# Query tiles 3 and 4 turned by way of DRAM and VectorE, and layer one's last blocks stored from ScalarE's queue

## The chip, the cores and the metric

The kernel runs on one core of a Trainium2 chip. Its time is the device time of one execution in microseconds. Engines are TensorE (PE, with its weight loads PEld), VectorE (DVE), ScalarE (ACT), GpSimd (POOL) and SyncE (SP). SP, ACT and POOL each have a queue from which they issue DMAs.

## The reference, cut to what matters

Two layers, each an attention block and a gated MLP, with the same weights in both. S = 2048 rows, D = 512, H = 32 heads of 16, Fh = 896; everything is float32.

```python
def _A_ref(x, wqkv, wo):                       # linear attention
    q, k, v = ...                              # heads of x @ wqkv
    phi = lambda t: jnp.where(t > 0, t + 1, jnp.exp(t)) + 1e-6
    pq, pk = phi(q), phi(k)
    kv = jnp.einsum("bhsd,bhse->bhde", pk, v)
    z = jnp.einsum("bhsd->bhd", pk)
    num = jnp.einsum("bhqd,bhde->bhqe", pq, kv)
    den = jnp.einsum("bhqd,bhd->bhq", pq, z)[..., None] + 1e-6
    return heads_joined(num / den) @ wo
def _B_ref(x, w_in, w_sp, b_sp, w_out):        # gated MLP over the sequence
    z = _gelu(jnp.einsum("bsd,df->bsf", x, w_in))
    z1 = z[..., :Fh]; z2 = _layernorm(z[..., Fh:], axis=-1)
    g = jnp.einsum("ts,bsf->btf", w_sp, z2) + b_sp[None, :, None]
    return jnp.einsum("bsf,fd->bsd", z1 * g, w_out)
x = x + _A_ref(_layernorm(x), ...)
x = x + _B_ref(_layernorm(x), ...)
x = x + _A_ref(_layernorm(x), ...)
x = x + _B_ref(_layernorm(x), ...)
```

## The kernel before

The sequence is cut into 16 tiles of 128 rows. A float32 product is made of three faster ones: every operand is split into a high part (an ACT copy, `high`, L220) and a low part (a VectorE subtraction, `low`, L223), and `mm3` (L234 to L236) multiplies high by high, high by low and low by high. So each product waits first for high parts and, from the second or third matmul on, for low parts.

Each layer L has four stages: P1 (keys, queries, the sums over the sequence), P2 (steps `s` over the tiles: the attention's output, the second layer norm, the MLP's first product), P4 (the product with `w_sp`, in seven sub-products P1 to P7 after Strassen) and the product with `w_out`. "Layer one" is L = 0 and "layer two" L = 1.

The order of each engine's instructions is the order in which the code issues them; there is no scheduler. Buffers are pools of numbered slots (`pages` of 128 x 512, 22 of them; `quads`; `bigs`; PSUM `banks`), handed out first in, first out. A DMA's queue also keeps order: an issue that waits holds back all behind it on its engine.

Query tiles pass through `Turn`, the class that transposes a tile. In P2, step s makes `a2_mul(s + 2)` (the divided queries, L877), stores that tile into the turn (`store`), and `b_high(s)` takes the turned tile out again, splits it, and `c(s)` multiplies it one step later. `c2` (L911) adds the product to x; `c3` stores x (L917) and normalises it (L378). `d_high`, `d_low` turn and split the normalised x tile in the same way, and `e` multiplies it.

A turn has two ways. For tiles in `by_pe`, ACT copies the tile with its features regrouped (L421), and TensorE transposes it in four matmuls against an identity into a PSUM bank (L390). For the others SP stores the tile into DRAM (L426), SP loads it in another order (L202, issued by `qturn.load`), and VectorE transposes 32 x 32 blocks into a page (L455). `by_pe` of the query turn also decides which steps of `run` and `run2` take the first branch of the step (those with the late query products of stage P1 in them).

At the end of P2, `tail` computes the last blocks of the activated half z1 (`out`, L1151: a GELU on ACT, then a store of the block, L1153) in three groups of three, and `yield`s between them; P4 starts in those gaps: at each yield it splits a weight block of `w_sp` (`wsp`: L1775 on ACT, L1778 on VectorE) and the z operand (L1883 or L220), and its products are L2000 to L2002. The store's engine is the argument `by`; without it, it is SP in layer one and POOL in layer two.

Of the kernel before, what the change touches and what calls it, by code (L numbers as in the profile page):

```python
# [19 lines left out]
NT = S // P  # L20
# [138 lines left out]
def mixer_kernel(ctx: ExitStack, tc: tile.TileContext, x_in, wqkv, wo_d, win1_d, win2_d, wsp_d, bsp_d, wout_d,  # L159
                 ident_d, mask_d, out_d):  # L160
    nc = tc.nc
# [76 lines left out]
    class Weight:  # L238


        def __init__(self, slots, shape, pieces, turned=False):
            self.slots, self.shape, self.pieces, self.turned = slots, shape, pieces, turned
            self.h = self.l = None
            self.raw = deque()
            self.n_load = self.n_split = 0
# [40 lines left out]
    def w_in1():  # L286
        return Weight(bigs, [P, NF, 4, P], [win1_d[f] for f in range(NF)])
# [543 lines left out]
    class P2:  # L831
        def __init__(self, p1):
            self.L = L = p1.L
            self.p1 = p1
            self.win1, self.win2 = None if L else w_in1(), p1.win2
            self.ws = deque()
            self.wf = deque([] if not L else [w1parts[f] for f in list(range(NF)) * 2 + [0, 6, 1, 2, 6]]
                            + [w1sums[f, m] for m in range(2) for f in range(3)]
                            + [[t[:, 256:512] for t in w1parts[f + 3]] for f in range(3)])
            self.draw, self.S, self.fdone, self.qhome, self.zacc, self.meant = {}, {}, None, {}, {}, set()  # L840
            self.qturn, self.xturn = Turn(f"qt{L}", range(5), True), Turn(f"yt{L}", (0, 1, 2, 3, NT - 1), home=ZHome, copy=bool(L))
            self.qp, self.qT, self.x, self.ms, self.xB, self.z, self.zms = {}, {}, {}, {}, {}, {}, {}
            self.fq = deque()
            self.fnext = []
            self.A, self.u, self.y = {}, {}, {}
# [388 lines left out]
        def tail(self):  # L1234
            V, A = nc.vector, nc.scalar.activation
            h, l = (t.bitcast(F32) for t in self.xT[3])
            L = self.L
            big = [bigs.get([P, NF, 512], F32R if k < 2 else F32) for k in range(3 if L else 2)]
            if L:
                c = [big[2][:, f] for f in range(3)]  # L1240
                room = Rooms(big[2][:, f] for f in range(3, NF))
            else:
                c = [pages.get(PAGE) for _ in range(3)]
                room = pages
# [13 lines left out]
            ws, d = [], []  # L1258
# [40 lines left out]
                V.tensor_add(c[f], d[f], c[f])  # L1299
            yield  # L1300
            for f in range(3):
                self.out(3, f + 3, c[f], c[f])
            x = [t[:, 2:4] for t in self.xT[3]]
            for f in range(3):
                self.fmul(self.y[f], [t[:, 256:512] for t in ws[f]], x, False, True)
# [1 line left out]
            quads.put(*self.xT.pop(3))  # L1307
            yield
            for f in range(3):
                self.out(3, f, self.y[f], room)  # L1310
                banks.done(self.y[f])
            for i in (NT - 2, NT - 1) if L else ():
                _, rs, nb = self.zms.pop(i)
# [7 lines left out]
                self.win1.free()  # L1321
            yield
            for f in range(3):
                self.out(2, f + 3, d[f], by=nc.sync)
                banks.done(d[f])
            bigs.put(*big)
            if not L:
# [2 lines left out]
        def run(self, sums):  # L1330
# [4 lines left out]
            for s in range(1, NT + 3):  # L1335
                if s in (15, 16, 17):
                    self.first_a(s - 15)
                self.loadx(s + 1)
                if s in self.qturn.by_pe:
                    self.c(s - 1)  # L1340
                    self.b_high(s)
                    self.c2(s - 1)
                    self.p1.late_phi_b()
                    self.b_low(s)
                    if s >= 2:
                        self.d_high(s - 2)
                        self.d_low(s - 2)
                    self.p1.late()
                    self.c3(s - 1)
                    self.a2(s + 2)  # L1350
                    self.p1.late_phi_a()
                    self.a(s + 3)
                    sums.tick()
                else:
                    if s < NT:
                        self.b_high(s)
                    self.a2_den(s + 2)
                    if s < NT:
                        self.b_low(s)
                    if s <= NT:  # L1360
                        self.c(s - 1)
                        self.c2(s - 1)
                    if s == NT:
                        quads.put(*self.W2)
                        pages.put(self.zbc)
                    self.a2_mul(s + 2)
                    late = s - 2 in self.xturn.by_pe and s <= NT or AHEAD <= s <= NT
                    if s in (NT, NT + 1):
                        self.e(s - 3)
                        self.e2(s - 3)  # L1370
                    if late:
                        self.d_high(s - 2)
                        self.d_low(s - 2)
                    if s <= NT:
                        self.c3(s - 1)
                    self.a(s + 3)
                    if s <= NT + 1 and not late:
                        self.d_high(s - 2)
                        self.d_low(s - 2)
# [99 lines left out]
        def run2(self):  # L1479
            late = self.p1  # L1480
            for s in range(1, NT + 3):
# [2 lines left out]
                self.qturn.load(s + 1)  # L1484
                if s in EXTRA:
                    self.wfetch()
                if s in self.qturn.by_pe:
                    self.c(s - 1)
                    self.b_high(s)
                    self.c2(s - 1)  # L1490
# [988 lines left out]
```

## Time and profile before

| | |
|---|---|
| median of 3 runs | 1342.88 us (1342.65 to 1342.91) |
| the profiled execution's own time | 1341.83 us |
| its span, first to last instruction | 1340.1 us |
| TensorE busy | 1334.2 us (100%), 6533 matmuls |
| VectorE busy | 1074.3 us (80%) |
| ScalarE busy | 739.8 us (55%) |
| GpSimd busy | 464.1 us (35%) |
| SP's and ACT's DMAs, share of 16 DMA engines | 56.2% |

Times in a row of a timeline are its start in us from the span's start, then its duration; "x8" behind it means eight merged instructions, and square brackets hold the idle time of the engine before it and what ended it. A row of grouped forms gives line, engine, operation, output<-input, form, count, busy us, mean ns of one, and idle time before. A row of waits gives the total, the number of times and the longest. Matmuls overlap: their durations are longer than the step from one start to the next, so the steps are read from the starts.

### The profile page before, as it was taken

The page shows a single profiled execution, that of the slowest core. Times are in us where ns is not written, and L with a number is a line of the kernel's source. Part 1 is how long each engine was busy: PE and PEld are TensorE (multiplying, and loading weights), DVE is VectorE, ACT ScalarE, POOL GpSimd, SP SyncE. Part 2 cuts the span into 40 slices and gives each one's busy share as a digit, 9 for nine tenths or more (in the row PEclk, how much of TensorE's full clock was granted, in tenths as well). Part 3 has the DMA queues.
Part 4 walks back from the last instruction along what each step waited for, and adds up shares of the span by engine and source line. Part 5 has one row for each costly group of instructions (what it writes and reads, how often), then busy time and mean ns, then how long its engine had stood idle before and what let it go on. Part 6 is the DMA issues. An engine that isn't in the chain of part 4 may idle for free.

```text
span 1340.1 us, 19243 instructions
## 1 busy us (share of the span) xinstructions
PE 1334.2 (100%) x6533; PEld 1138.6 (85%) x6533; DVE 1074.3 (80%) x1687; ACT 739.8 (55%) x1250; POOL 464.1 (35%) x611
## 2 busy tenths in 40 slices
PE   9999999999999999999999999999999999999998
PEld 7888888888888888889988888888888888888898
DVE  7779877767899889898866777777689758899885
ACT  5774544347742265345666655557687333666464
POOL 3765675533036400301422443544441012122021
PEclk9999999999999999999999999999999999999999
DMA  5898489977779986884864552678767455579354
GB/s 184 281 313 275 166 286 313 306 223 250 250 270 378 324 263 216 287 302 79 184 159 138 137 131 88 211 237 269 226 203 246 155 171 174 178 242 322 115 78 65
DMA packets 172594, 291.34 MB, mean 217 GB/s; under 512 B 14544, under 2 KB 53456, under 8 KB 172240
## 3 DMA queue, kind: packets, MB, share of 16 engines
q1 hardware_dynamic: 153376, 250.92, 56.2%
q0 software_dynamic: 18976, 39.07, 13.7%
q8 instruction: 51, 0.84, 0.3%
q14 instruction: 47, 0.39, 0.1%
q10 hardware_dynamic: 144, 0.13, 0.0%
HBM read 205.39 MB, written 101.45 MB: 229 GB/s over the span
## 4 chain that ended last, share of the span: by engine, by line
PE 95%; DMA 2%; DVE 2%; ACT 1%; issue 0%; POOL 0%; SPq 0%; DVEq 0%; ACTq 0%
PE bank L234 13%; PE bank L236 13%; PE bank L235 13%; PE bank L2001 12%; PE bank L2000 12%; PE bank L2002 12%; PE bank L2198 3%; PE bank L2199 3%; PE bank L2200 3%; PE bank L990 1%; PE bank L991 1%; PE bank L992 1%; PE bank L1163 1%; PE bank L1162 1%; PE bank L1161 1%; PE bank L390 1%
## 5 line engine op out<-in xcount | busy, mean ns | idle before, releaser
L2001 PE MATMUL bank<-qd,pg 128*128 128x512 f32 x736 | 286.5, 389 | 0.6 <-DVE qd L1778 0.6
L2002 PE MATMUL bank<-qd,pg 128*128 128x512 f32 x736 | 286.3, 389 | 0.0
L2000 PE MATMUL bank<-qd,pg 128*128 128x512 f32 x736 | 286.3, 389 | 0.0
L1775 ACT ACTIVATE qd<-qd 128x1024 fp32r<-128x1024 f32 x142 | 149.2, 1053 | 125.2 <-PE bank L2002 101.7
L1778 DVE TENSOR_TENSOR qd<-qd,qd 128x1024 fp32r<-128x1024 f32 x132 | 168.6, 1279 | 37.6 <-ACT qd L1775 37.4
L236 PE MATMUL bank<-qd,pg 128*128 128x512 f32 x448 | 174.7, 390 | 0.0
L2001 PEld LDWEIGHTS bank<-qd,pg 128*128 128x128 f32 x736 | 138.1, 188 | 29.5 <-DVE qd L1778 1.0
L2002 PEld LDWEIGHTS bank<-qd,pg 128*128 128x128 f32 x736 | 138.1, 188 | 28.8
L2000 PEld LDWEIGHTS bank<-qd,pg 128*128 128x128 f32 x736 | 138.1, 188 | 28.6
L2041 POOL TENSOR_TENSOR bg<-bg,pg 128x512 f32<-128x512 f32 x28 | 49.8, 1780 | 187.6 <-ACT qd L1775 92.5
L234 PE MATMUL bank<-qd,pg 128*128 128x512 f32 x264 | 103.2, 391 | 0.3 <-ACT pg L220 0.2
L235 PE MATMUL bank<-qd,pg 128*128 128x512 f32 x264 | 102.9, 390 | 0.0
L236 PEld LDWEIGHTS bank<-qd,pg 128*128 128x128 f32 x448 | 84.1, 188 | 18.2 <-DVE pg L223 0.4
L1684 POOL TENSOR_TENSOR pg<-pg,pg 128x512 f32<-128x512 f32 x48 | 70.8, 1476 | 68.7 <-DMA pg<-in_wsp_dram 66.6
L369 POOL TENSOR_SCALAR rs<-mv 128x1 f32<-128x1 f32 x76 | 23.8, 313 | 172.7 <-DVE mv L367 169.0
L2200 PE MATMUL bank<-wo,qd 128*128 128x256 f32 x288 | 81.5, 283 | 0.0
L2198 PE MATMUL bank<-wo,qd 128*128 128x256 f32 x276 | 78.1, 283 | 0.0
L2199 PE MATMUL bank<-wo,qd 128*128 128x256 f32 x276 | 78.0, 283 | 0.0
L220 ACT ACTIVATE pg<-pg 128x512 fp32r<-128x512 f32 (+1 forms) x86 | 50.0, 592 | 45.8 <-DVE pg L1869 19.9
L223 DVE TENSOR_TENSOR pg<-pg,pg 128x512 fp32r<-128x512 f32 (+1 forms) x84 | 54.5, 657 | 11.3 <-ACT pg L220 10.6
L549 POOL TENSOR_TENSOR pg<-pg,pg 128x512 f32<-128x512 f32 x30 | 39.9, 1331 | 55.8 <-DVE pg L543 53.9
L234 PE MATMUL bank<-bg,qd 128*128 128x448 f32 x160 | 59.0, 369 | 0.0
(297 smaller groups left out, 3358.2 us busy)
## 6 DMA issues: line engine op xcount, KB each, us to landing
qd<-s SPq DMA_DIRECT2D x62, 512.0 KB, 4.6
qd<-in_wsp_dram SPq DMA_DIRECT2D x40, 512.0 KB, 4.0
qd<-hP SPq DMA_DIRECT2D x40, 512.0 KB, 4.6
pg<-z SPq DMA_DIRECT2D x56, 256.0 KB, 5.1
pg<-in_wsp_dram SPq DMA_DIRECT2D x52, 256.0 KB, 4.4
s<-pg SPq DMA_DIRECT2D x48, 256.0 KB, 4.0
z<-pg SPq DMA_DIRECT2D x40, 256.0 KB, 3.5
pg<-w POOLq DMA_DIRECT2D x38, 256.0 KB, 4.9
```

Source lines behind the costliest of these rows:

```text
L234: nc.tensor.matmul(out, ah, bh, start=start, stop=False)
L235: nc.tensor.matmul(out, ah, bl, start=False, stop=False)
L236: nc.tensor.matmul(out, al, bh, start=False, stop=stop)
L1684: nc.gpsimd.tensor_tensor(t, a, b, op=OP.add)
L1775: self.mark = nc.scalar.activation(w[:, 0], r, AF.Copy)
L1778: nc.vector.tensor_sub(w[:, 1], r, w[:, 0].bitcast(F32))
L2000: m(out, h[:, o], w[:, 0, j, :], start=start, stop=False, skip_group_check=True)
L2001: m(out, h[:, o], w[:, 1, j, :], start=False, stop=False, skip_group_check=True)
L2002: m(out, l[:, o], w[:, 0, j, :], start=False, stop=stop, skip_group_check=True)
L2198: m(out, A, x, start=start and f == 0, stop=False, skip_group_check=True)
L2199: m(out, A, y, start=False, stop=False, skip_group_check=True)
L2200: m(out, B, x, start=False, stop=stop and f == 2, skip_group_check=True)
```

## The change

The query turn's `by_pe` goes from tiles 0 to 4 to tiles 0 to 2 in both layers. The two loops' branch, which hung on `by_pe`, now hangs on `s < 5` (the last pair of lines below, in `run` and in `run2`), so the steps keep their order. In layer one, all nine stores of the tail are issued by ACT in place of SP; layer two keeps POOL and SP.

```diff
-            self.qturn, self.xturn = Turn(f"qt{L}", range(5), True), ...
+            self.qturn, self.xturn = Turn(f"qt{L}", range(3), True), ...
...
             for f in range(3):
-                self.out(3, f + 3, c[f], c[f])
+                self.out(3, f + 3, c[f], c[f], None if L else nc.scalar)
...
-                self.out(3, f, self.y[f], room)
+                self.out(3, f, self.y[f], room, None if L else nc.scalar)
...
-                self.out(2, f + 3, d[f], by=nc.sync)
+                self.out(2, f + 3, d[f], by=nc.sync if L else nc.scalar)
...
-                if s in self.qturn.by_pe:
+                if s < 5:
```

Three places show what moves. In the rows, `pg`, `qd`, `bg` are slots of pages, quads and bigs with running numbers; `qt_3` is the DRAM tile of query tile 3, `x_0` the stored x tile 0, `s_...` stored sums of `w_sp`, `z_0_2_3` a stored block of z1.

VectorE in layer one, step 3, from `a2_mul(4)` on, before:

```order
L877 SCALAR_TENSOR_TENSOR pg_196_1754<-z_q_674,den 128x512
L911 TENSOR_TENSOR pg_191_1693<-pg_191_1693,bank_69_1856 128x512
L365 BN_STATS st<-pg_191_1693 128x6
L367 BN_AGGR mv<-st 128x2
L531 SCALAR_TENSOR_TENSOR z_q_1839<-bank_68_1816,z_q_1839 128x512
L223 TENSOR_TENSOR pg_211_1887<-bank_70_1869,pg_210_1874 128x512
```

and with the change:

```order
L877 SCALAR_TENSOR_TENSOR pg_195_1754<-z_q_674,den 128x512
L455 STREAM_TRANSPOSE pg_210_1873<-pg_199_1766 128x4x128
L911 TENSOR_TENSOR pg_191_1693<-pg_191_1693,bank_69_1860 128x512
L365 BN_STATS st<-pg_191_1693 128x6
L367 BN_AGGR mv<-st 128x2
L531 SCALAR_TENSOR_TENSOR z_q_1841<-bank_68_1818,z_q_1841 128x512
L223 TENSOR_TENSOR pg_212_1888<-pg_210_1873,pg_211_1875 128x512
```

The transpose of tile 3 stands between the divided queries of tile 4 and the addition L911, and L223 reads its page in place of a bank.

SP in layer one, from the store of x tile 0 on, before:

```order
L917 DMA x_0_79<-pg_170_1518 128x512
L1679 DMA s_145<-pg_175_1542 128x512
L1679 DMA s_2_131<-pg_174_1540 128x512
L202 DMA pg_197_1758<-in_wsp_dram 128x512
L202 DMA pg_198_1760<-in_wsp_dram 128x512
L202 DMA pg_199_1762<-in_wsp_dram 128x512
L202 DMA pg_200_1770<-in_win_dram 128x512
L202 DMA pg_201_1772<-in_x_dram 128x512
L917 DMA x_1_80<-pg_171_1520 128x512
```

and with the change:

```order
L917 DMA x_0_79<-pg_170_1518 128x512
L426 DMA qt_3_1749<-pg_188_1673 128x4x128
L1679 DMA s_145<-pg_175_1542 128x512
L1679 DMA s_2_131<-pg_174_1540 128x512
L202 DMA pg_196_1758<-in_wsp_dram 128x512
L202 DMA pg_197_1760<-in_wsp_dram 128x512
L202 DMA pg_198_1762<-in_wsp_dram 128x512
L202 DMA pg_199_1766<-qt_3_1749 128x512
L202 DMA pg_200_1772<-in_win_dram 128x512
L202 DMA pg_201_1774<-in_x_dram 128x512
L917 DMA x_1_80<-pg_171_1520 128x512
L426 DMA qt_4_1839<-pg_195_1754 128x4x128
```

Tile 3's store now stands ahead of two stores of sums and three loads, and its load ahead of the next loads and of the store of x tile 1; tile 4's store follows.

ACT in layer one's tail, the third group of blocks, before:

```order
L1151 ACTIVATE pg_374_3939<-bank_146_3792 128x512
L1151 ACTIVATE pg_375_3943<-bank_147_3801 128x512
L1151 ACTIVATE pg_376_3947<-bank_148_3810 128x512
L220 ACTIVATE pg_378_3954<-pg_371_3929 128x512
L220 ACTIVATE pg_381_3965<-pg_377_3951 128x512
L1775 ACTIVATE qd_26_3984<-qd_22_3825 128x1024
L220 ACTIVATE pg_383_3987<-pg_380_3962 128x512
```

and with the change:

```order
L1151 ACTIVATE pg_376_3937<-bank_144_3790 128x512
L1153 DMA z_0_2_3_3939<-pg_376_3937 128x512
L1151 ACTIVATE pg_377_3941<-bank_145_3799 128x512
L1153 DMA z_0_2_4_3943<-pg_377_3941 128x512
L1151 ACTIVATE pg_378_3945<-bank_146_3808 128x512
L1153 DMA z_0_2_5_3947<-pg_378_3945 128x512
L220 ACTIVATE pg_380_3952<-pg_373_3927 128x512
L220 ACTIVATE pg_383_3963<-pg_379_3949 128x512
L1775 ACTIVATE qd_26_3982<-qd_22_3823 128x1024
L220 ACTIVATE pg_385_3985<-pg_382_3960 128x512
```

Each of the three activations is followed by the issue of its own store on ACT; the next z operands (L220) and the next weight (L1775) stand behind them. Before, SP issued these stores.

More of the change, by code (lines that the diff above doesn't have):

```diff
@@ L840, in __init__ @@
             self.draw, self.S, self.fdone, self.qhome, self.zacc, self.meant = {}, {}, None, {}, {}, set()
-            self.qturn, self.xturn = Turn(f"qt{L}", range(5), True), Turn(f"yt{L}", (0, 1, 2, 3, NT - 1), home=ZHome, copy=bool(L))
+            self.qturn, self.xturn = Turn(f"qt{L}", range(3), True), Turn(f"yt{L}", (0, 1, 2, 3, NT - 1), home=ZHome, copy=bool(L))
             self.qp, self.qT, self.x, self.ms, self.xB, self.z, self.zms = {}, {}, {}, {}, {}, {}, {}
@@ L1486, in run2 @@
                     self.wfetch()
-                if s in self.qturn.by_pe:
+                if s < 5:
                     self.c(s - 1)
```

## The prediction

> **What bounds the kernel now.** I read the page first (its span, busy times, slices and the shares of the chain that ended last), then the waits of TensorE alone, then the timelines round the two places of the change.
>
> ```profile
> span 1340.1 us, 19243 instructions
> PE   9999999999999999999999999999999999999998
> PEclk9999999999999999999999999999999999999999
> PE 95%; DMA 2%; DVE 2%; ACT 1%; issue 0%; POOL 0%; SPq 0%; DVEq 0%; ACTq 0%
> ```
>
> TensorE is at work in every slice at the full granted clock, and 95% of the chain lies on it. So a microsecond taken out of its stream is a microsecond of the end, and any other engine matters only where TensorE comes to wait for it.
>
> ```profile
> PE bank L619 <- DVE ones_f L185: 1.0, 1, 1.0
> PE bank L2001 <- DVE qd L1778: 0.6, 1, 0.6
> ```
>
> These are the two longest of four recorded waits of TensorE in the span. The first is the start. The second lies at 354 us, in the stretch where layer one's last activated blocks are stored, so the second half of the change can touch it.
>
> **What the removed transposes are worth.** The forms of the operations, then TensorE's timeline in layer one:
>
> ```profile
> L390 PE MATMUL bank<-ident,pg 128*128 128x128 f32 x84 | 11.7, 273 | 0.5 <-DVE pg L380 0.5
> 157.45 1.03 PE L390 MATMUL bank<-ident,pg 128*128 128x128 f32 x8
> 158.24 0.45 PE L234 MATMUL bank<-bg,qd 128*128 128x448 f32 x1
> 163.19 0.40 PE L234 MATMUL bank<-qd,pg 128*128 128x512 f32 x1
> 174.41 0.60 PE L390 MATMUL bank<-ident,pg 128*128 128x128 f32 x4
> 174.77 0.45 PE L234 MATMUL bank<-bg,qd 128*128 128x448 f32 x1
> ```
>
> From start to next start, eight transposes (a query tile and an x tile) take 158.24 - 157.45 = 0.79 us, and four (an x tile alone) 174.77 - 174.41 = 0.36. The change turns eight into four at four places, two tiles in each of two layers: 4 x 0.43 = 1.7 us out of a stream that does not wait. The busy time of the first row agrees: 11.7 / 84 = 0.139 each, x 16 = 2.2; I take 1.7, since starts are what the stream advances by. Four ACT copies (L421) fall away too; they lie beside TensorE's work and count as nothing, and the four bank evacuations now read SBUF.
>
> **What the new path costs in layer one.** A tile goes VectorE (L877), SP store, SP load, VectorE transpose (L455), ACT high part, VectorE low part (L223). Tile 3's first product is the L234 row at 163.19, which comes 0.43 earlier once its transposes are gone: high part due at 162.8, low part (third product) at 163.2. The timelines of VectorE and SP as they stand, then three rows of the page's DMA issues (KB each, us to landing) and the form of L455:
>
> ```profile
> 150.06 1.33 DVE L877 SCALAR_TENSOR_TENSOR pg<-z_q,den 128x512 f32<-128x512 f32 x1
> 156.83 1.43 DVE L877 SCALAR_TENSOR_TENSOR pg<-z_q,den 128x512 f32<-128x512 f32 x1
> 158.19 0.68 DVE L911 TENSOR_TENSOR pg<-pg,bank 128x512 f32<-128x512 f32 x1
> 161.12 0.69 DVE L223 TENSOR_TENSOR pg<-bank,pg 128x512 fp32r<-128x512 f32 x1 [0.32 <-ACT pg L220]
> 146.50 0.88 SPq L1679 DMA_DIRECT2D s<-pg  x2
> 147.47 1.70 SPq L202 DMA_DIRECT2D pg<-in_wsp_dram  x3
> 152.01 0.33 SPq L917 DMA_DIRECT2D x<-pg  x1
> pg<-x SPq DMA_DIRECT2D x32, 256.0 KB, 3.1
> qt<-pg SPq DMA_DIRECT2D x22, 256.0 KB, 2.6
> pg<-qt SPq DMA_DIRECT2D x22, 256.0 KB, 3.4
> L455 DVE STREAM_TRANSPOSE pg<-pg 128x512 f32<-128x512 f32 x22 | 23.7, 1078 | 5.6 <-ACT pg L1093 2.9 <-DMA qt<-pg 2.4 <-DMA x<-pg 0.2
> ```
>
> Tile 3 is ready to store at 150.06 + 1.33 = 151.4. The store stands on SP ahead of the two sum stores and three weight loads that now issue at 146.50 and 147.47, so SP stands still from 146.5 to 151.4 and these five come some 5 us later. POOL's sums read those loads, and one step of look-ahead covers the delay. The store lands at about 154.1 (2.6), the load behind the five issues at about 154.9 and lands at about 158.4 (3.4). L455's output page is also the one that the store of x tile 1 reads (the row at 152.01), and that store now follows the load on SP: issued near 156, landed near 159. VectorE reaches L455 at 156.83 + 1.43 = 158.26, so it waits 0.2 to 1.2 us, transposes for 1.08, and only then runs L911 (now at 158.19), the statistics and L531. L223, now at 161.12, moves to about 162.6 and ends near 163.2: at the edge. I charge 0.3 us, between 0 (a landing that beats VectorE) and 1.5 (both transfers a microsecond late). Tile 4 has the same route; its store waits for the second L877 row, its load lands near 165, and VectorE gets there only after 167. Its L223 ends some 0.4 us before its product: 0, up to 0.5.
>
> L223 also changes its operands from bank and page to two pages:
>
> ```profile
> L223 DVE TENSOR_TENSOR pg<-bank,pg 128x512 fp32r<-128x512 f32 x30 | 20.3, 678 | 2.3 <-ACT pg L220 2.1
> L223 DVE TENSOR_TENSOR pg<-pg,z_q 128x512 fp32r<-128x512 f32 x22 | 22.6, 1027 | 6.3 <-ACT z_q L220 6.3
> ```
>
> The later tiles, which already go this way, take 1.03 us against 0.68: up to 0.35 more, inside the 1.5 above. The Trainium skill ("SBUF — State Buffer", "SBUF: two separate sides") says that VectorE with two SBUF inputs and a GpSimd instruction lock each other out of a shared port for a whole instruction. The two rows agree with that direction; by the page a low part could lose a whole POOL addition, and the sum would be about a microsecond smaller a tile.
>
> **Layer two** has no sums on SP and more room:
>
> ```profile
> 828.14 0.69 DVE L911 TENSOR_TENSOR pg<-pg,bank 128x512 f32<-128x512 f32 x1 [0.95 <-PE bank L236]
> 836.62 0.69 DVE L911 TENSOR_TENSOR pg<-pg,bank 128x512 f32<-128x512 f32 x1 [3.08 <-PE bank L236]
> ```
>
> VectorE idles 0.95 and 3.08 us exactly where the two L455 (1.08 each) now stand: 0 charged, up to 0.3.
>
> **The stores on ScalarE's queue.** Layer one's tail in the timelines of ACT, VectorE, TensorE and SP, with the landings of its stores, ACT's one DMA issue of the whole trace, and a stretch of 5 us (its last numbers are the clock, the DMA share and GB/s):
>
> ```profile
> 338.95 1.66 ACT L1151 ACTIVATE pg<-pg 128x512 f32<-128x512 f32 x3
> 344.98 1.70 ACT L1151 ACTIVATE pg<-bank 128x512 f32<-128x512 f32 x3
> 352.09 0.63 ACT L220 ACTIVATE pg<-pg 128x512 fp32r<-128x512 f32 x1 [1.31 <-DMA z<-pg]
> 352.63 1.04 ACT L1775 ACTIVATE qd<-qd 128x1024 fp32r<-128x1024 f32 x1
> 353.71 1.23 DVE L1778 TENSOR_TENSOR qd<-qd,qd 128x1024 fp32r<-128x1024 f32 x1 [0.26 <-ACT qd L1775]
> 354.99 0.50 PE L2001 MATMUL bank<-qd,pg 128*128 128x512 f32 x1 [0.56 <-DVE qd L1778]
> 343.93 5.07 SPq L1153 DMA_DIRECT2D z<-pg  x6
> L2226 ACTq DMA_DIRECT2D out_dram<-pg x1: 369/369/369, 1335.7 to 1335.7; - x1
> DMA to landing us min/median/max: 4.4/5.4/6.1
> 345.88 0.39 PE L2000 MATMUL bank<-qd,pg 128*128 128x512 f32 x1
> 345.00:350.00 5.00, 5.00 (x24) 4.14 (x23) 1.90 (x3) 1.66 (x4) 0.00 (x0) 1.00 1.05 394
> ```
>
> The L220 at 352.09 writes the page that the first store of the third group read. It waits for that store's landing; then follow weight 3's high part (L1775), its low part (L1778) and TensorE's L2001, which starts 0.95 us after its predecessor where 0.23 is the rule: 0.7 us lost. SP issues the last six stores in 5.07 us, with landings of 4.4 to 6.1 us (the landing row is that of the nine stores) while the DMA engines are full (share 1.05).
>
> With the change each store stands behind its activation on ACT, which must end first: an activation's 0.59 plus 0.05 plus an issue of 0.37 (ACT's only issue so far) to 0.45 makes 1.07 in place of 0.52, 1.6 us later for each group of three, 4.9 for all nine. The three groups then start at 338.95, 343.8 and 348.5 and the last ends near 351.8. TensorE asks for the low part of weight n at 345.88 + 0.23 + 2.72 n (12 products of 0.227 each). Weight 1 ends near 345.1 and weight 2 near 349.9 (351.6 is when it is asked for), so both stay ahead. Weight 3 is the one that stalls now. The first store of the third group issues near 349.2; spread over 12 us in place of 8, I take a landing in 3 us (2.6 when the queue is quiet, 5.4 when it is full). Then L220 starts at 352.4, L1778 ends near 355.2 in place of 354.94, and the next weight, whose page waits for the ninth store, is ready about 0.3 us after TensorE asks. Charge: +0.6. Below: if the issue runs beside ACT's work, the 0.7 stall goes. Above: landings of 5.4 give +3.0 (rivals). SP gains nine slots, and its next loads can go when their buffers are free; none of them is waited for by TensorE.
>
> The sum: -1.7 + 0.3 + 0 + 0 + 0.6 = -0.8 us. The profiled execution took 1341.83 (span 1340.1); the median of the runs is 1342.88. I put the -0.8 on the median: 1342.1.
>
> **The rivals.**
> Everything is covered and the stall at 354 goes: -1.7 - 0.7 = -2.4, 1340.5. For it: the stores leave as soon as their blocks exist. Against: ACT's two back-to-back groups leave no room for nine issues.
> The stores land no sooner: L220 waits until 349.2 + 5.4 = 354.6, L1778 ends at 357.5, 2.5 us later than now, and the next weight costs 0.5 more: -1.7 + 0.3 + 3.0 = +1.6, 1344.5. For it: the 5.4 us row; against: the wider spread. The Trainium skill ("DMA: Bandwidth & Descriptors", "Rules for kernel authors") says that spreading DMAs over queues brings no bandwidth and saves only the time to issue. By that rule this rival holds; the row with share 1.05 agrees that the engines, not SP, were full.
> Slower: ACT's issue costs what SP's does there, 5.07 / 6 = 0.85, and landings stay at 5.4. A store then adds about 0.92 to ACT; the third group starts at 350.5, its first store issues by 351.1 and lands at 356.5, L1778 ends near 359.4 (+4.5), and the next weight, behind the ninth landing near 359.6, costs 1.3 more: -1.7 + 0.3 + 5.8 = +4.4, 1347.3. It decides from an issue of about 0.6 us on. Against: ACT's own row, 0.37.
> Tile 3 of layer one late: L455 waits 2 us for its load or for the page's store, TensorE stands for about 2: +0.9, 1343.8.
>
> **How the numbers follow.** Chances: forecast 0.50, all covered 0.17, landings late 0.15, slow issue 0.10, tile 3 late 0.08. 0.2% (2.7 us) is about what a measurement of this kernel can tell from no change. Only the slow issue passes it upwards, with the tails of the two late cases: 0.13. Downwards the all-covered case ends just short: 0.06. Same: 0.81. The range reaches from all covered, 1340.4, to the late landings with 0.7 us of a late tile 3, 1345.2; it leaves out the slow issue.
>
> **What would show it.** Right: four transposes at every one of the four places, 0.36 us from start to start; L455 of tile 3 waiting under 1.2 us for a DMA; ACT's issues near 0.4 us; one stall of TensorE near 354, 0.5 to 1.5 us, behind L1778. Wrong: TensorE waiting for ACT or VectorE at tile 3's product, ACT's queue issues above 0.6 us, L220 in the tail waiting for z stores beyond 353, or any new wait elsewhere, since all pages rotate differently.

## The result, and the profile after

The change makes the kernel slower: 1350.2 us (median of 6 runs, 1349.1 to 1351.8) against 1342.9 for the kernel before, a ratio of 1.0053 with a 95% interval of 1.004 to 1.0066, or 5.4 to 8.9 us. The forecast was 1342.1. The profiled execution took 1351.47 us, its span is 1349.6.

First lines of the changed kernel's page, and five of the ten waits recorded for TensorE (total, times, longest):

```profile
span 1349.6 us, 19228 instructions
PE   9999999999899999999999999999999999999998
PE 78%; DVE 6%; DMA 6%; ACT 3%; POOL 3%; issue 2%; SPq 1%; ACTq 0%; DVEq 0%; POOLq 0%
```

```profile
PE bank L2001 <- DVE qd L1778: 3.4, 1, 3.4
PE bank L236 <- DVE pg L223: 1.9, 3, 0.8
PE bank L619 <- DVE ones_f L185: 1.0, 1, 1.0
PE bank L2000 <- ACT pg L1838: 0.7, 1, 0.7
PE bank L2000 <- DVE bg L2058: 0.4, 1, 0.4
```

One slice of TensorE fell to 8, and TensorE's share of the chain that ended last fell from 95% to 78%: those of VectorE and the DMAs grew from 2% to 6%, those of ScalarE and GpSimd to 3%. The wait for the weight's low part (L1778) grew from 0.6 to 3.4 us, waits behind a query tile's low part (L223) are new, and so are two waits for products late in layer one.

**Layer one, steps 2 to 4.** Before, ScalarE's high part and VectorE's low part of tile 2 waited for no DMA:

```profile
153.63 0.58 ACT L220 ACTIVATE pg<-bank 128x512 fp32r<-128x512 f32 x1
154.30 0.69 DVE L223 TENSOR_TENSOR pg<-bank,pg 128x512 fp32r<-128x512 f32 x1 [0.37 <-ACT pg L220]
```

With the change, the timelines of TensorE, SP, ACT and VectorE (start, duration, form, idle time before and what ended it):

```profile
156.94 0.50 PE L236 MATMUL bank<-qd,pg 128*128 128x512 f32 x1 [0.75 <-DVE pg L223]
159.35 0.60 PE L390 MATMUL bank<-ident,pg 128*128 128x128 f32 x4
159.71 0.45 PE L234 MATMUL bank<-bg,qd 128*128 128x448 f32 x1
166.33 0.50 PE L236 MATMUL bank<-qd,pg 128*128 128x512 f32 x1 [0.79 <-DVE pg L223]
146.65 0.33 SPq L917 DMA_DIRECT2D x<-pg  x1
152.03 0.38 SPq L426 DMA_DIRECT2D qt<-pg  x1
152.50 0.94 SPq L1679 DMA_DIRECT2D s<-pg  x2
156.80 0.38 SPq L917 DMA_DIRECT2D x<-pg  x1
154.81 0.60 ACT L220 ACTIVATE pg<-bank 128x512 fp32r<-128x512 f32 x1 [3.38 <-DMA qt<-pg]
156.20 0.69 DVE L223 TENSOR_TENSOR pg<-bank,pg 128x512 fp32r<-128x512 f32 x1 [2.11 <-DMA s<-pg]
162.51 1.13 DVE L455 STREAM_TRANSPOSE pg<-pg 128x512 f32<-128x512 f32 x1 [2.19 <-DMA x<-pg]
```

The transposes went as forecast: four in place of eight, 0.36 us from start to start. But SP issued nothing from 146.65 + 0.33 to 152.03, until VectorE had made tile 3 (its L877 ended at 151.97), and the two stores of sums behind it left at 152.50 in place of 146.50. Each store reads a page that is next in the list. ScalarE's high part of tile 2 waited 3.38 us for the page of tile 3's own store; VectorE's low part of tile 2 waited 2.11 us for the page of a sum's store, and TensorE for it. Then the transpose of tile 3 waited 2.19 us for the page of x tile 1, whose store had slipped from 152.01 to 156.80. Tile 2 is a tile that the change does not touch.

**Layer one's tail.** The third group on ACT, VectorE, TensorE, and the landings of the nine stores:

```profile
353.46 0.58 ACT L1151 ACTIVATE pg<-bank 128x512 f32<-128x512 f32 x1
354.07 0.33 ACTq L1153 DMA_DIRECT2D z<-pg  x1
355.42 0.33 ACTq L1153 DMA_DIRECT2D z<-pg  x1
356.50 0.33 ACTq L1153 DMA_DIRECT2D z<-pg  x1
361.81 0.63 ACT L220 ACTIVATE pg<-pg 128x512 fp32r<-128x512 f32 x1 [2.78 <-DMA z<-pg]
361.21 0.69 DVE L223 TENSOR_TENSOR pg<-pg,pg 128x512 fp32r<-128x512 f32 x1 [2.26 <-DMA z<-pg]
361.82 1.22 DVE L1778 TENSOR_TENSOR qd<-qd,qd 128x1024 fp32r<-128x1024 f32 x1
363.09 0.50 PE L2001 MATMUL bank<-qd,pg 128*128 128x512 f32 x1 [3.40 <-DVE qd L1778]
```

```profile
DMA to landing us min/median/max: 2.9/4.8/5.7
```

VectorE's L223, the low part of a z operand, writes the page that the eighth store reads. It was issued at 355.42 and landed 5.7 us later, and the weight's low part L1778 stands behind L223 on VectorE. So TensorE waited 3.4 us.

### The profile page after: what moved, and what is told of

Its sections match the earlier page's. It is cut to its first block, busy times and chain, and to the rows that moved or that the text cites. A ratio compares the mean times of both kernels' runs of the same rounds, so it can differ in the third digit from the quotient of the medians.

```text
span 1349.6 us, 19228 instructions
## 1 busy us (share of the span) xinstructions
PE 1337.3 (99%) x6517; PEld 1136.0 (84%) x6517; DVE 1079.0 (80%) x1691; ACT 738.4 (55%) x1246; POOL 463.2 (34%) x611
## 4 chain that ended last, share of the span: by engine, by line
PE 78%; DVE 6%; DMA 6%; ACT 3%; POOL 3%; issue 2%; SPq 1%; ACTq 0%; DVEq 0%; POOLq 0%
PE bank L2001 11%; PE bank L2000 11%; PE bank L2002 11%; PE bank L236 8%; PE bank L234 8%; PE bank L235 8%; PE bank L2198 3%; PE bank L2199 3%; PE bank L2200 3%; DMA s<-pg 1%; DMA x<-pg 1%; DVE st L365 1%; PE bank L990 1%; PE bank L992 1%; PE bank L991 1%
## 5 line engine op out<-in xcount | busy, mean ns | idle before, releaser
L1775 ACT ACTIVATE qd<-qd 128x1024 fp32r<-128x1024 f32 x142 | 149.2, 1053 | 126.1 <-PE bank L2002 84.5
L1778 DVE TENSOR_TENSOR qd<-qd,qd 128x1024 fp32r<-128x1024 f32 x132 | 168.4, 1278 | 39.8 <-ACT qd L1775 39.7
L2001 PEld LDWEIGHTS bank<-qd,pg 128*128 128x128 f32 x736 | 138.2, 188 | 32.3 <-DVE qd L1778 3.8
L2000 PEld LDWEIGHTS bank<-qd,pg 128*128 128x128 f32 x736 | 138.2, 188 | 30.8 <-ACT pg L1838 1.1
L2002 PEld LDWEIGHTS bank<-qd,pg 128*128 128x128 f32 x736 | 138.2, 188 | 28.9 <-DVE pg L1840 0.3
L236 PEld LDWEIGHTS bank<-qd,pg 128*128 128x128 f32 x448 | 84.1, 188 | 21.3 <-DVE pg L223 3.9
L220 ACT ACTIVATE pg<-pg 128x512 fp32r<-128x512 f32 (+1 forms) x90 | 52.6, 594 | 54.9 <-DVE pg L1869 20.1
L223 DVE TENSOR_TENSOR pg<-pg,pg 128x512 fp32r<-128x512 f32 (+1 forms) x88 | 57.0, 657 | 12.9 <-ACT pg L220 10.1
L234 PEld LDWEIGHTS bank<-qd,pg 128*128 128x128 f32 x264 | 49.6, 188 | 12.0 <-ACT pg L220 1.2
```

The source lines that it names most:

```text
L234: nc.tensor.matmul(out, ah, bh, start=start, stop=False)
L236: nc.tensor.matmul(out, al, bh, start=False, stop=stop)
L1775: self.mark = nc.scalar.activation(w[:, 0], r, AF.Copy)
L1778: nc.vector.tensor_sub(w[:, 1], r, w[:, 0].bitcast(F32))
L2000: m(out, h[:, o], w[:, 0, j, :], start=start, stop=False, skip_group_check=True)
L2001: m(out, h[:, o], w[:, 1, j, :], start=False, stop=False, skip_group_check=True)
```

## The experiments

The time of each run is the ratio to the kernel before with its interval (in us, times 1342.7). Beside it, from TensorE's starts, I add up for a stretch by how much its steps exceed the median step of the same line, where that is over 0.06 us; this also counts small waits that the list leaves out, and steps at a low clock, and it moves by some 0.3 us with how like steps are grouped. The stretches are P2's first part (148 to 250 us), the tail (348 to 375), and late P4 (450 to 485). The expectations speak of differences of medians, the table of ratios. Three runs of one execution each are not in the table; only their waits and landings are read.

| run | ratio (95%) | us | P2 | tail | late P4 |
|---|---|---|---|---|---|
| before | | | 0.6 | 0.8 | 0 |
| the change | 1.0053 (1.004 to 1.0066) | +7.1 | 5.2 | 3.7 | 1.7 |
| turning alone | 1.002 (1.0012 to 1.0029) | +2.7 | 4.3 | 0.4 | 5.0 |
| stores alone | 1.0036 (1.0024 to 1.0048) | +4.8 | 0.9 | 6.6 | 0 |
| turning, layer two | 0.9992 (0.9984 to 1.0001) | -1.1 | 0.6 | 0.8 | 0 |
| turning, layer one | 1.0031 (1.0019 to 1.0043) | +4.2 | 4.5 | 0 | 0 |
| layer one, tile 4 alone | 1.0024 (1.0014 to 1.0033) | +3.2 | 2.2 | 0.7 | 1.8 |
| layer one, stores later | 1.0009 (1.0 to 1.0019) | +1.2 | 2.4 | 0.1 | 0 |
| stores, other pages | 1.0007 (0.9997 to 1.0016) | +0.9 | 0.6 | 1.0 | 0 |
| pages shifted only | 1.0006 (0.9996 to 1.0015) | +0.8 | 0.6 | 0.1 | 2.8 |
| layer two and pages | 0.9992 (0.9983 to 1.0) | -1.1 | 0.6 | 0 | 0.2 |
| both layers, repaired | 0.9989 (0.998 to 0.9998) | -1.5 | 1.8 | 0 | 0.2 |
| the change, repaired | 1.0003 (0.9994 to 1.0013) | +0.4 | 1.4 | 1.4 | 0.2 |

The theory was that stores come to land later, and that the writers of their pages wait; the rivals were ScalarE's time, VectorE's added work, and the shifted order of the pages. The first four runs take the change apart.

**Turning alone.** The three edits of the tail's stores undone:

```diff
-                self.out(3, f + 3, c[f], c[f], None if L else nc.scalar)
+                self.out(3, f + 3, c[f], c[f])
...
-                self.out(2, f + 3, d[f], by=nc.sync if L else nc.scalar)
+                self.out(2, f + 3, d[f], by=nc.sync)
```

> Only the turning of tiles 3 and 4 by way of DRAM, in both layers; the tail's stores stay on SP. Theory (SP's ordered queue holds stores of sums and of x behind tile 3's store in layer one, and writers of the freed pages wait for them): TensorE keeps the three waits behind VectorE's low parts near 157, 166 and 183 us (1.9 us recorded in the change, some 3.9 with the small gaps), the wait in the tail near 355 us falls back from 3.4 to about 0.6; time = before - 1.7 + 3.9 = +2.2 us, and up to +3.6 if the two waits near 470 us (1.4) belong to the turning. Rival (the stores on ScalarE alone cost the time): -1.7 us, no wait of TensorE in layer one between 150 and 190 us.

+2.7 us, inside the theory's 2.2 to 3.6; the waits near 157 and 166 us are there, 0.8 and 0.9 us, and the tail's wait is 0.2. The rival's -1.7 falls. This profile is of the slowest of its runs (1350.4 us, the median is 1345.5) and holds a wait of 3.2 us near 467 us, taken up with the shifted pages below.

**Stores alone.**

```diff
-            self.qturn, ... = Turn(f"qt{L}", range(3), True), ...
+            self.qturn, ... = Turn(f"qt{L}", range(5), True), ...
```

> Only the nine stores of layer one's tail on ScalarE's queue; all five query tiles are turned on TensorE as before, so pages are handed out in the order of before. Theory (the third group's stores land late, and VectorE's low part of the z operand, which stands ahead of the weight's low part, waits for their pages): one wait of TensorE near 355 us of about 3.4 us in place of 0.6, time +2.8 us, no new wait in 150 to 330 us. Rival one (the stores cost all): +7 to +9 us. Rival two (the shifted order of the pages made the wait in the tail, not the queue): the wait stays at 0.6 us and the time within 0.5 us of before.

The wait came as expected, 3.6 us in one place and nothing in P2, with every page where it was before: so the change of queue brings it, not the shifted order of the pages. But the time is +4.8, not +2.8. The stretches of 5 us of this run show why (busy time and count of PE, PEld, DVE, ACT, POOL; then the granted clock, the DMA share and GB/s):

```profile
355.00:360.00 5.00, 1.91 (x5) 1.53 (x6) 3.12 (x4) 3.30 (x7) 0.00 (x0) 0.70 0.20 23
360.00:365.00 5.00, 5.00 (x16) 3.92 (x15) 5.00 (x11) 3.98 (x6) 0.00 (x0) 0.62 0.80 244
365.00:370.00 5.00, 5.00 (x24) 4.14 (x23) 5.00 (x8) 3.14 (x5) 0.00 (x0) 1.00 0.69 179
```

Behind the wait TensorE runs on a granted clock of 0.62: 16 matmuls in 5 us in place of 24. That is 2.8 of the tail's 6.6 us; the wait is the other 3.8.

**Turning in layer two, and in layer one.**

Both on SP's stores, first this, then the same with the two ranges exchanged:

```diff
-            self.qturn, ... = Turn(f"qt{L}", range(3), True), ...
+            self.qturn, ... = Turn(f"qt{L}", range(3) if L else range(5), True), ...
```

> Turning by way of DRAM for tiles 3 and 4 in layer two alone; layer one and the stores as before. Theory: layer two has the room, so the eight transposes fall out of a stream that does not wait: -0.86 us, no new wait of TensorE after 680 us. Rival (any change of the order of the pages makes waits somewhere): 0 to +2 us with new waits after 810 us.

> Turning by way of DRAM for tiles 3 and 4 in layer one alone; layer two and the stores as before. Theory: -0.86 + 3.9 = +3.0 us, with waits of TensorE behind VectorE's low parts near 157, 166 and 183 us, and up to +4.4 if the two waits near 470 us come with it. Rival (the stores on ScalarE cost the time): -0.86 us and no such waits.

Layer two alone: -1.1 us (-2.1 to +0.1, so not told from nothing), no new wait at its steps. Layer one alone: +4.2, with the waits near 157, 166 and 183 us; the rival's -0.86 falls. The parts add up: 2.7 + 4.8 = 7.5 us against the change's 7.1.

**The queue, or VectorE's work?** In the next run layer one's two stores move behind the store of an x tile of the following step; `qstore` is the store with the put of its page, taken out of `a2_mul` for tiles 3 and 4.

```diff
                     self.c3(s - 1)
+                    if s in (2, 3):
+                        self.qstore(s + 1)
+                    if s == 3:
+                        self.qturn.load(4)
                     self.a2(s + 2)
...
+                if s == 2:
+                    self.qturn.load(3)
                 self.qturn.load(s + 2)
```

> Layer one alone turns tiles 3 and 4 by way of DRAM (the run that came out 3.6 us slower), with one thing altered: SP issues each of the two stores one step later, behind the store of the x tile of that step, and tile 3's load behind the next sums, so that no store of a sum and no store of an x tile stands behind a query tile that is not ready. VectorE's work is the same as in that run. Theory (the loss is the stores that SP holds back and the pages that are not free until they land): the waits behind low parts near 157, 166 and 183 us (1.8 us recorded) go, time before - 0.9 us. Rival (VectorE's added work, two transposes of 1.08 us and low parts of 1.03 in place of 0.68, is what makes its low parts late): the waits stay and the time is before + 2 to + 3.6 us.

VectorE's work is the same, and the loss falls from 4.2 to 1.2 us, P2's excess from 4.5 to 2.4. VectorE in P2 of this run:

```profile
153.87 0.68 DVE L223 TENSOR_TENSOR pg<-bank,pg 128x512 fp32r<-128x512 f32 x1
160.40 1.11 DVE L455 STREAM_TRANSPOSE pg<-pg 128x512 f32<-128x512 f32 x1 [1.75 <-DMA pg<-qt]
```

Tile 2's low part waits for nothing now, where it waited 2.11 us, and TensorE's first wait is gone. What stays in its place is new: tile 3's load, now issued at 156.3, lands at 160.4, and TensorE waits 0.3 us for its low part near 164 us (0.5 by its steps), and 0.3 again near 181 us. So VectorE's work is not the cause of the first waits; "all waits go" was too much, and 1.8 us of P2's excess stay.

**The page, or ScalarE's time?** With all nine stores on ScalarE, the first group's three pages are put back ahead of the third group's instead of behind:

```diff
             yield
+            if not L:
+                pages.put(*c)
             for f in range(3):
                 self.out(2, f + 3, d[f], by=nc.sync if L else nc.scalar)
...
-            if not L:
-                pages.put(*c)
```

> The nine stores of layer one's tail on ScalarE's queue (the run that came out 5.2 us slower), with one thing altered: the three pages of the first group are put back into the list ahead of the third group's, not behind, so that the next operands of z write pages whose stores are long landed. Queue, order and landings stay. Theory (VectorE's low part of z, which waits for a store of the third group to land, holds the weight's low part behind it): the wait of 3.6 us near 354 us goes, and with it the low clock behind it; time before - 0.7 to + 0.3 us. Rival (ScalarE, with an issue behind each activation, has no time left and is late itself): the wait stays at 2 us or more, time +2 to +5 us.

VectorE and the wait in this run:

```profile
353.33 0.68 DVE L223 TENSOR_TENSOR pg<-pg,pg 128x512 fp32r<-128x512 f32 x1
353.94 1.22 DVE L1778 TENSOR_TENSOR qd<-qd,qd 128x1024 fp32r<-128x1024 f32 x1
```

```profile
PE bank L2001 <- DVE qd L1778: 0.7, 1, 0.7
```

Same queue, same issues (the last at 350.96, against 350.94), other pages: the wait falls from 3.6 to 0.7, the clock stays at 1.00, and +4.8 becomes +0.9 (-0.4 to +2.1). So ScalarE's own time is in these 0.9 us (at most 2.1), and the waiting for pages makes the rest.

**Which stores are late, and why.** Two runs with all tiles turned on TensorE and part of the stores on ScalarE. First the third group's three go back to SP:

```diff
-                self.out(2, f + 3, d[f], by=nc.sync if L else nc.scalar)
+                self.out(2, f + 3, d[f], by=nc.sync)
```

> The first six stores of the tail on ScalarE's queue, the third group's three on SP's. Theory (the delay adds up over the groups: 1.6 us for each, since an activation waits for the issue ahead of it): the third group's stores issue from about 348.8 us on as with all nine, end about 0.9 us earlier, and TensorE waits 2 to 3.2 us near 354 us (3.6 with all nine, 0.6 before). Rival (only the third group's own issues on ScalarE matter): the wait is 0.6 to 1 us.

Then the first six in place of these:

```diff
-                self.out(3, f + 3, c[f], c[f], None if L else nc.scalar)
+                self.out(3, f + 3, c[f], c[f])
...
-                self.out(3, f, self.y[f], room, None if L else nc.scalar)
+                self.out(3, f, self.y[f], room)
```

> Only the third group's three stores of the tail on ScalarE's queue, the first six on SP's. Theory (the delay adds up over the groups): the third group starts at 345 us as before, its stores issue from 345.6 to 348 us, about as on SP's queue, and TensorE's wait near 354 us is 0.3 to 1.2 us. Rival (only the third group's own issues on ScalarE matter): 3 us or more.

Both came out the other way (one execution each, 1343.7 and 1346.3 us; the median of the kernel before was 1342.6). With the third group on SP TensorE waits 0.9 us; with only the third group on ScalarE it waits in three places, 2.8 us of excess in all. The wait does not add up over groups. What differs is SP's next load, 512 KB of a weight (`qd<-in_wsp_dram`): behind SP's own stores it has to wait for them; beside ScalarE's it does not. SP, and the landings of all nine stores, in the second run:

```profile
348.78 8.29 SPq L1754 DMA_DIRECT2D qd<-in_wsp_dram  x2
```

```profile
DMA to landing us min/median/max: 4.4/6.0/7.7
```

The load left at 348.8, ahead of the last store (349.9), which landed 7.7 us later. To test it, the change's stores with only the ninth on SP, so that this load stands behind it:

```diff
-                self.out(2, f + 3, d[f], by=nc.sync if L else nc.scalar)
+                self.out(2, f + 3, d[f], by=nc.sync if L or f == 2 else nc.scalar)
```

> The nine stores of the tail on ScalarE's queue, but for the ninth, which is on SP's; the pages as in the change. SP's next load of a weight, 512 KB, then stands behind the ninth store, where with all nine on ScalarE it is issued at 349.6 us, in the middle of the third group. Theory (stores of the third group that are issued after this load share the DMA engines with it and land in 5.7 to 7.8 us; those ahead of it in 3 to 5): the eighth store lands in at most 4.8 us, and TensorE waits 0.8 to 2 us near 354 us in place of 3.6. Rival (it is the later issue and the other queue that make these stores late): 3 us or more.

SP and VectorE, then the landings of the seventh and eighth (median) and of the ninth:

```profile
351.35 0.33 SPq L1153 DMA_DIRECT2D z<-pg  x1
351.79 5.40 SPq L1754 DMA_DIRECT2D qd<-in_wsp_dram  x2
354.96 0.69 DVE L223 TENSOR_TENSOR pg<-pg,pg 128x512 fp32r<-128x512 f32 x1 [1.72 <-DMA z<-pg]
```

```profile
z<-pg ACTq DMA_DIRECT2D x2, 256.0 KB, 4.1
z<-pg SPq DMA_DIRECT2D x1, 256.0 KB, 4.1
```

The eighth store left at 350.27, later than in the run with all nine on ScalarE (349.86), and freed its page earlier, at 354.96 in place of 356.21; TensorE waited 1.7 us in place of 3.6. So, in this one execution (1344.0 us), 1.9 of the 3.6 us go with the place of the load that overtook. Of the other 1.7 the kernel before had 0.6; that the later issue makes the rest is argued, not shown. The Trainium skill ("DMA: Bandwidth & Descriptors", "Queues, rings and completion order") says that a DMA engine goes round the queues that have work, packet by packet; the landings here agree with that.

**Tile 4 alone.**

```diff
-            self.qturn, ... = Turn(f"qt{L}", range(5) if L else range(3), True), ...
+            self.qturn, ... = Turn(f"qt{L}", range(5) if L else range(4), True), ...
```

> Layer one alone, and of it tile 4 alone, turned by way of DRAM; tile 3 on TensorE, the tail's stores on SP. Theory (tile 3's store, which is 5 us later than the stores of sums that it holds back, makes the first two waits, near 156 and 165 us; tile 4's makes what follows): those two waits of 0.9 us are not there, a wait of 0.2 to 1 us stands near 165 us or later, time before - 0.4 to + 1 us. Rival (either tile's store holds SP back alike): +1.5 us or more.

The first two waits are gone, as expected of tile 3, but the time came out on the rival's side. Tile 4 holds SP back in the same way a step later: VectorE's low part of tile 3 waits for the page of tile 4's store. TensorE's steps show no loss there. Its wait comes near 180 us, behind VectorE's low part of tile 5; the last two rows are of VectorE and POOL just ahead of it:

```profile
162.43 0.69 DVE L223 TENSOR_TENSOR pg<-bank,pg 128x512 fp32r<-128x512 f32 x1 [1.98 <-DMA qt<-pg]
180.54 0.50 PE L236 MATMUL bank<-qd,pg 128*128 128x512 f32 x1 [0.53 <-DVE pg L223]
178.46 1.09 DVE L869 TENSOR_TENSOR den<-den,zeps 128x32 f32<-128x32 f32 x1
178.21 1.29 POOL L228 TENSOR_TENSOR bg<-pg,bg 128x512 fp32r<-128x512 f32 x1
```

From 168.27 us on VectorE has no pause, where the kernel before had two, of 0.94 and 1.78 us. What used them up is the wait of 1.98, the added transpose of 1.11, and two runs of the small L869 (1.17 and 1.09 us in place of 0.19), each of which ended within 0.1 us of an operation of POOL. In the run below that repairs both layers VectorE waits for no store's page between 160 and 180 us, and TensorE's wait there is still 0.3. So VectorE's added work has a part in the later waits of P2; how large a part is not shown.

P2 loses 1.6 us more than before, less 0.4 for the four transposes that fall away; the measured +3.2 (1.9 to 4.4) is more than that, and the profile's remainder lies near 465 us, in the wait of the next run. How often tile 4's kernel has that wait is open.

**The order of the pages alone.** The kernel before, with two pages taken and put back, so that from there on each page is that of the change:

```diff
                 self.qturn.load(s + 2)
+                if s == 4:
+                    pages.put(*[pages.get(PAGE) for _ in range(2)])
```

> The kernel before, with one thing added: after step 4 of layer one two pages are taken from the list and put back at once. No instruction is added; from there on every page is the one that the change uses (two takings further round the list). Theory (what costs the time is that stores come later, not which page stands where): within 0.6 us of before, and no wait of TensorE of over 0.3 us between 150 and 200 us or between 455 and 480 us. Rival (the order of the pages itself makes the two waits near 470 us, 0.5 and 0.85 us in the change, and the one near 197 us): those waits are there, and the time is 1 to 2 us above before.

P2 is that of before, to 0.1 us. The shift begins behind a load that SP issued at 177.2 us, so the order of the pages is not what makes the waits near 183 and 199 us; of those near 157 and 166 this run says nothing. The time is +0.8 (-0.5 to +2.0): not shown to differ. But the profile holds the two waits of late P4, 1.5 and 0.7 us, against the theory. The product's operand on VectorE, in the change and in this run (line numbers two higher):

```profile
464.35 4.54 DVE L1840 TENSOR_TENSOR pg<-pg,pg 128x384 fp32r<-128x384 f32 x1
466.55 1.92 POOL L2041 TENSOR_TENSOR bg<-bg,pg 128x512 f32<-128x512 f32 x1
```

```profile
457.17 4.54 DVE L1842 TENSOR_TENSOR pg<-pg,pg 128x384 fp32r<-128x384 f32 x1
```

```profile
PE bank L2002 <- DVE bg L2060: 1.5, 1, 1.5
```

VectorE's operation takes 4.54 us beside POOL's additions, where it takes 0.55 elsewhere; in the kernel before POOL's additions end at 457.97, and it starts at 458.06. Eight of this kernel's ten runs lie at 1342.3 to 1343.3 and two at 1345.0 and 1345.3; the profile is of one of the two. So this wait comes without any held store and, as the times suggest, in some executions only. It is in the change's profile (1.7 us); that the change causes it is not shown, nor that it does not make it more frequent.

**The repairs together.** First layer two's turning with SP's stores and the move of `pages.put(*c)` shown above:

> Layer two alone turns tiles 3 and 4 by way of DRAM, all stores of the tail are on SP as before, and the first group's three pages are put back ahead of the third group's (the edit that took the wait out of the run with the stores on ScalarE). Theory: -0.86 us for eight transposes in a stream that does not wait, and -0.5 to -0.7 us for the wait near 354 us that was there before: 1.2 to 1.6 us below before. Rival (the wait near 354 us has another cause than the pages, such as the weight's own load): the wait of 0.6 us stays, -0.86 us at most.

Then layer one turned as well, with `qstore` ahead of `c3` in place of behind it, and after it the same with the change's nine stores on ScalarE:

```diff
+                    if s in (2, 3):
+                        self.qstore(s + 1)
+                    if s == 3:
+                        self.qturn.load(4)
                     self.c3(s - 1)
-                    if s in (2, 3):
-                        self.qstore(s + 1)
-                    if s == 3:
-                        self.qturn.load(4)
```

> As the run before it, and layer one turns tiles 3 and 4 by way of DRAM too, with SP's stores of the two tiles one step later but ahead of the store of the x tile of that step (in the run with the later store tile 3's load landed at 160.4 us, VectorE waited 1.75 us for it and TensorE 0.5 us). Theory: tile 3's load lands a microsecond or more earlier, the wait near 162 us falls below 0.2 us, and layer one's turning gains 0 to 0.86 us on the run before it: 1.2 to 2.4 us below before. Rival (the route by way of DRAM is too long for these tiles in layer one wherever the store stands): the waits near 162 and 179 us stay at 0.4 us or more, time 0 to 1 us above the run before it.

> The change itself (both layers turn by way of DRAM, all nine stores of the tail on ScalarE's queue) with the two repairs: SP's stores of the two tiles of layer one stand behind the sums of the step before, and the first group's pages go back ahead of the third group's. Theory (held stores in layer one and the pages of the third group make the whole loss, and the parts add up): 7 us below the change, that is the run with the repairs and SP's stores (1.5 us below before) + 0.6 to 1.3 for a wait of 0.9 near 354 us: 0.2 to 1 us below before. Rival (something else in the change, such as ScalarE's issues or POOL's later sums, carries part of the loss): 1.5 us or more above before.

The wait in the tail that was there before is gone in the first (excess 0 against 0.8): -1.1 us, which is no more than layer two's turning gave alone. Turning layer one too gives -1.5 (-2.7 to -0.3), the only kernel here whose interval excludes no gain; the wait near 164 us is gone, one of 0.3 near 180 stays, and against the run ahead of it no difference can be told. The change itself with both repairs is at +0.4 (-0.8 to +1.7) in place of +7.1: the two repairs take out nearly all of the loss. Against the -1.7 of the transposes some 2 us stay: by the excess 0.8 in P2 and 0.6 in the tail, the rest is not placed.

## Why the prediction was wrong

- *Sixteen transposes, -1.7.* Right: 0.36 us for four at every place, and -1.1 (-2.1 to +0.1) measured for the half in layer two, -0.86 forecast.
- *Layer two, 0.* Right. The two L455 there waited for their loads, but no wait of TensorE follows.
- *Tile 3 in layer one, +0.3, at most 1.5.* This step failed. P2 lost 4.6 us more in the change, with tile 4's part in it. I followed tile 3 along its route: store, load, transpose, split. Most numbers on it came near: the store at 152.03 (151.4 + SP's turn), the stores of sums and loads behind it some 5 us late, L455 at the page of x tile 1. I then asked who reads those five transfers (POOL's sums) and not who writes the pages that the late stores read. The rows that settle it are ACT's L220 and VectorE's L223 of tile 2, with waits of 3.38 and 2.11. And VectorE's wait at L455 was 2.19 where 0.2 to 1.2 stood, since x tile 1's store left at 156.80 (156 forecast) and its page came free 5.7 us after that. The 3.1 taken for the landing is the row of loads from x (`pg<-x`); SP's stores into x took 4.0 in the median of the kernel before.
- *L223 on two pages, up to 0.35.* It took 0.68 us in these steps, not 1.03: nothing was lost there. POOL stretched other operations of VectorE, L869 in P2 and L1840 near 465 us.
- *Tile 4, 0.* Failed: 1.6 us in P2 by itself. Its store too holds SP back, which costs VectorE 1.98 us, and the sum left out that VectorE then has no pause left to catch up in.
- *The stores on ScalarE, +0.6.* The mechanism was right and its size wrong: 2.8 us in the change's tail, 5.8 in the stores' own run with the slow clock. The issue was cheaper than forecast (0.33 against 0.37) and a store's place on ScalarE nearly as forecast (354.79 to 355.87, 1.08 against 1.07). Two things failed. I let the third group's stores land in 3 us, since they are spread more widely, and did not ask what SP would issue in their place: the 512 KB load. And I took the first store's page, which ScalarE needs, for the one that decides. It was the eighth, which VectorE needs ahead of L1778 in its order. "None of them is waited for by TensorE", on SP's earlier loads, overlooked that they delay what is.
- *The rivals.* "The stores land no sooner" had the tail's size right (+3.0), though it too took the first store's page. The one for a late tile 3 had the right place and stopped at tile 3. "Slow issue" fell. That two of them could happen together, plus a slow clock, was in none.
- *"All pages rotate differently"* stood among the things that could make it wrong. By itself it costs nothing in P2 from 177 us on.

## What to carry to other kernels

When a DMA is put into an ordered queue ahead of others, price the stores behind it by the buffers that they hold: find who writes each one next, on every engine, not only who reads the data. When stores leave a queue, ask which large transfer moves up in it and shares the DMA engines with them. Where a landing is late in any case, buffers freed long ago, put ahead in the list, cost no instruction and took out nearly the whole stall.

## What the runs showed of the hardware

A stop of TensorE can cost more than its own length, where the granted clock is low behind it. After the wait of 3.6 us in the tail of the stores' own run the clock was 0.62 for the next 5 us (rows above). After the 3.2 us near 467 us of the run that turns alone:

```profile
465.00:470.00 5.00, 1.83 (x9) 1.22 (x8) 5.00 (x5) 0.00 (x0) 2.46 (x3) 1.00 1.06 263
470.00:475.00 5.00, 5.00 (x17) 3.94 (x16) 4.61 (x9) 1.48 (x2) 0.11 (x1) 0.66 1.05 259
```

After the 3.4 us in the change's profile it was not low:

```profile
360.00:365.00 5.00, 1.91 (x8) 1.60 (x9) 3.01 (x4) 3.19 (x7) 0.00 (x0) 1.00 0.28 51
365.00:370.00 5.00, 5.00 (x23) 4.13 (x23) 5.00 (x11) 4.09 (x6) 0.00 (x0) 1.00 0.83 225
```

The Trainium skill ("TensorE: Matmul & The Clock Gate", "What's actually happening") gives a window of about 3.4 us without work, running on its own, after which the clock is halved. The trace agrees in part: a window that runs on its own can pass over one of three stops of nearly that length, but the shortest wait, 3.2 us, lies under it (its matmuls start 3.6 us apart). The waits of 1.7 us (ninth store on SP) and 1.5 us (pages shifted) left the clock at 1.00.
